# Block products for four more groups of joint tiles, and ScalarE durations by form in a kernel's list scheduler

## The chip, the cores and the metric

One core of a Trainium2 chip. The time is device microseconds of one execution, given as the median of several; the program runs on a single core, and every run used here is recorded as a fast one, with a granted TensorE clock of 0.997 to 1.00. A profile is of one execution of its own; its span is about 2 us shorter than that execution's time.

## The reference, cut to what matters

```python
B, T, D, K, U = 2, 4000, 512, 5, 8
h  = gelu(conv(x, w1))[:, ::2, :]          # 5 taps, stride 2
f  = gelu(conv(h, w2))[:, ::2, :]          # 5 taps, stride 2: 1000 rows a batch
fe = f @ w_f ;  ge = g @ w_g
j  = tanh(fe[:, :, None, :] + ge[:, None, :, :])
out = j @ w_o                              # 2 x 1000 x 8 rows of 512
```

The last product has 16,000 rows. The kernel does it in 125 **joint tiles** of 128 rows, in between and after the second batch's convolutions.

## The kernel before

The kernel first writes down all operations in program order; a **list scheduler** then orders them per engine by estimated durations. A plain joint tile is four matmuls of 512 columns into one PSUM bank, an eviction by VectorE or ScalarE, and a store issued by the sync engine:

```python
def act(o, i, func, scale=1.0, bias=None, cost=None):
    ...
    pl.op("act", ..., cost or o.ap.free_size() * 0.83e-3 + 0.13)      # the scheduler's duration
...
def joint_tile(jt):
    c0 = jt * P
    ahead(c0 + P, 900)                      # tanh of the columns to come
    ...
    early = jt < U * T2 // P                # tiles 0..61
    s = jt % 4 if early else 4 + jt % NSLOT # store slot, each with its own semaphore
    for h in range(2 if last else 1):       # the last tile in two halves
        ...
        mm(v, [(j(k), wo_sb[k, cl]) for k in range(NK)], True, True)
        if h == 1 or (jt % 3 == 2 if early else jt % 6 == 5) and not last:
            act(o, v, ACT.Copy)             # eviction on ScalarE
        else:
            ...                             # eviction on VectorE
        send(c0, s, cl, ("sp", "act")[h])
```

Eight **groups** of four tiles in the tail (tiles 64 and up) are done by seven instead of eight products of 2 x 2 blocks: `sums` makes four combinations of the operand (here on POOL), and four steps do two, two, two and one product, each of four matmuls of 256 columns. A group takes three of the eight PSUM banks in its first step.

```python
def one():
    held.extend(banks.pop(0) for _ in range(3))
    x, y, z = held
    product(Ab(0, 0), Bb(0, 0), x, True)
    product(Sb(1), Tb(1), y, True)
    act(k1, v2(x), ACT.Copy)
    tt("dve", u2, v2(y), k1, add)
...
WQ = (16, 18, 20, 22, 24, 26, 28, 30)       # the groups; a plain tile follows each of their steps
while todo and todo[0] < 60:                # plain tiles that run before the first group
    joint_tile(todo.pop(0))
```

At the end the sync engine waits for the semaphore of each of the 16 store slots.

## Time and profile before

| | |
|---|---|
| time, median | 266.12 us (265.56 to 266.48) |
| span of the profiled execution | 264.1 us |
| TensorE busy | 256.8 us, 97% |
| VectorE, ScalarE busy | 207.1 and 184.3 us |
| first joint tile's weight load | 88.90 us |
| start of the last eviction | 260.31 us |

The prediction below shows the page, the chain and the windows. Two views also belong here. The first is the list of waits of TensorE's weight loads between 150 and 258 us (columns: who waited for whom, us in total, times, longest):

```profile
PEld acc L424 <- DVE ostq L411: 0.9, 2, 0.5
PEld acc L424 <- ACT kq L416: 0.4, 2, 0.2
PEld acc L424 <- issue: 0.2, 1, 0.2
```

Here the weight loads ran ahead of the matmuls, so not all of the 1.3 us of the first two lines is lost; the starts of the matmuls show 0.47 us of lost time at 215.2, 218.2, 222.0 and 238.1 us. The second is the timeline of the end (start, length, what):

```profile
258.59 1.69 PE L424 MATMUL acc<-wo_sb,jL 128*128 128x512 bf16 x11
259.87 0.42 DVE L1059 CAST ostq<-acc 128x256 bf16<-128x256 f32 x1 [0.39 <-PE acc L424]
260.31 0.38 ACT L416 ACTIVATE ostq<-acc 128x256 bf16<-128x256 f32 x1 [0.28 <-DVE ostq L1059]
...
257.49 4.15 SPq L1038 DMA_DIRECT2D out_dram<-ostq  x8
```

The sync engine issues eight stores until 261.64 us with hardly a pause; the last ones begin 0.48 to 0.49 us apart. Store issue lags behind the evictions there.

### The profile page before, as it was taken

To read this page: it belongs to the slowest core of one execution; us is meant where nothing else is said; L and a number is where in the kernel's file an instruction comes from. 1 tells how busy PE (TensorE), PEld (TensorE's weight loads), DVE (VectorE), ACT (ScalarE), POOL (GpSimd) and SP (SyncE) were. 2 spreads that over 40 slices of the span, in tenths; PEclk is the share of its full clock that TensorE was granted. 3 is DMA by queue.
4 is the path that set the end of the run, shared out by engine and by line. 5 is a ranking of instruction groups with operands and counts; after the bars stand their busy time and mean duration, and the time that the engine had idled before them with its cause. 6 is when DMAs were issued, how large, how long until landed. Compare 5 with 4: busy or idle time off the path is not lost.

```text
span 264.1 us, 4593 instructions
## 1 busy us (share of the span) xinstructions
PE 256.8 (97%) x1658; PEld 161.3 (61%) x1678; DVE 207.1 (78%) x379; ACT 184.3 (70%) x305; POOL 43.3 (16%) x52
## 2 busy tenths in 40 slices
PE   8999999999999899999999999999999999999994
PEld 4887764456666555655655545555665666666662
DVE  0999999999999999994324999854345687887883
ACT  2788979984466999567547578738449999996111
POOL 1000005100000000000000000000003979698000
PEclk9999999999999999999999999999999999999998
DMA  6999998979993021211111113321101354445445
GB/s 239 327 180 218 293 260 147 171 128 194 227 183 62 20 83 58 79 40 62 41 60 40 63 60 119 123 80 60 61 21 40 123 159 159 161 142 179 160 160 159
DMA packets 56708, 33.94 MB, mean 129 GB/s; under 512 B 31582, under 2 KB 56430, under 8 KB 56686
## 3 DMA queue, kind: packets, MB, share of 16 engines
q1 hardware_dynamic: 54430, 31.49, 44.9%
q0 software_dynamic: 2112, 2.10, 4.6%
q8 instruction: 13, 0.21, 0.4%
q14 instruction: 9, 0.07, 0.1%
q10 hardware_dynamic: 144, 0.07, 0.1%
HBM read 7.86 MB, written 16.38 MB: 92 GB/s over the span
## 4 chain that ended last, share of the span: by engine, by line
PE 79%; DVE 14%; ACT 3%; issue 2%; DVEq 0%; ACTq 0%
PE acc L424 78%; DVE wide L411 2%; DVE r L592 2%; DVE r32b L592 2%; ACT w_t L416 1%; DVE ws L592 1%; DVE hT L411 1%; ACT jT L416 1%; PE acc L517 1%; DVE feT L988 1%; DVE sd L592 1%; DVE wide L741 1%; DVE row L592 1%; DVE row L741 1%; DVE acc L592 1%
## 5 line engine op out<-in xcount | busy, mean ns | idle before, releaser
L424 PE MATMUL acc<-wo_sb,jT 128*128 128x512 bf16 x242 | 60.5, 379 | 1.4 <-ACT jT L416 0.7
L1059 DVE CAST ost<-acc 128x512 bf16<-128x512 f32 x42 | 28.8, 688 | 19.6 <-PE acc L424 18.2
L416 ACT ACTIVATE jT<-feT,geT 128x1000 bf16<-128x1000 f32 (+9 forms) x56 | 40.9, 777 | 3.9 <-PE acc L424 2.4
L424 PEld LDWEIGHTS acc<-wo_sb,jT 128*128 128x128 bf16 x256 | 24.9, 98 | 23.8 <-ACT jT L416 0.8
L424 PE MATMUL acc<-wo_sb,jL 128*128 128x512 bf16 (+1 forms) x178 | 36.0, 336 | 0.3
L416 ACT ACTIVATE jL<-feT,geT 128x1000 bf16<-128x1000 f32 (+3 forms) x36 | 34.6, 1030 | 0.6 <-DVE feT L988 0.6
L1096 POOL TENSOR_TENSOR sA<-jL 128x512 f16<-128x512 bf16 x16 | 18.5, 1156 | 94.4 <-ACT jL L416 94.2
L424 PEld LDWEIGHTS acc<-wo_sb,jL 128*128 128x128 bf16 x184 | 17.8, 98 | 10.5 <-ACT kq L416 0.4
L424 PE MATMUL acc<-xt,w_sb 128*128 128x252 bf16 (+1 forms) x144 | 23.5, 305 | 0.0
L416 ACT ACTIVATE sd<-acc 128x334 f32<-128x334 f32 (+1 forms) x32 | 13.8, 443 | 11.8 <-PE acc L424 11.6
L416 ACT ACTIVATE hT<-acc 128x334 bf16<-128x334 f32 (+3 forms) x33 | 15.1, 464 | 9.1 <-PE acc L424 9.0
L1059 DVE CAST ostq<-acc 128x512 bf16<-128x512 f32 (+1 forms) x26 | 17.5, 678 | 4.1 <-PE acc L424 4.0
L424 PE MATMUL acc<-row,w_sb 128*128 128x334 bf16 (+1 forms) x112 | 20.5, 305 | 0.0
L424 PEld LDWEIGHTS acc<-xt,w_sb 128*128 128x128 bf16 x144 | 14.0, 98 | 7.0 <-DVE xt L411 0.3
L424 PE MATMUL acc<-zx,w_sb 128*128 128x334 bf16 (+1 forms) x96 | 17.6, 305 | 0.0
L411 DVE TENSOR_TENSOR ostq<-acc,kq 128x512 bf16<-128x512 f32 x24 | 15.7, 682 | 1.6 <-PE acc L424 1.6
L411 DVE TENSOR_TENSOR sd<-sd 128x334 f32<-128x334 f32 (+1 forms) x16 | 8.0, 503 | 10.7 <-ACT sd L416 10.7
L416 ACT ACTIVATE ost<-acc 128x512 bf16<-128x512 f32 x20 | 11.8, 592 | 5.0 <-PE acc L424 4.7
L424 PEld LDWEIGHTS acc<-row,w_sb 128*128 128x128 bf16 x112 | 10.9, 98 | 6.2
L424 PE MATMUL acc<-row,w_t 128*128 128x334 bf16 (+1 forms) x80 | 14.6, 305 | 0.0
L424 PE MATMUL acc<-xs,w_t 128*128 128x252 bf16 (+1 forms) x76 | 14.0, 314 | 0.3 <-issue 0.3
L416 ACT ACTIVATE ostq<-acc 128x512 bf16<-128x512 f32 (+1 forms) x14 | 8.2, 589 | 8.7 <-PE acc L424 8.2
(105 smaller groups left out, 469.1 us busy)
## 6 DMA issues: line engine op xcount, KB each, us to landing
out_dram<-ost SPq DMA_DIRECT2D x55, 128.0 KB, 1.9
out_dram<-ostq SPq DMA_DIRECT2D x54, 128.0 KB, 2.0
w_sb<-in_w_dram SPq DMA_DIRECT2D x10, 512.0 KB, 5.8
xr<-in_x_dram SPq DMA_DIRECT2D x2, 512.0 KB, 4.0
half<-w_sb POOLq DMA_DIRECT2D x2, 512.0 KB, 6.4
half<-w_t POOLq DMA_DIRECT2D x2, 512.0 KB, 5.2
wf_sb<-in_w_f_dram SPq DMA_DIRECT2D x1, 512.0 KB, 6.9
wg_sb<-in_w_g_dram SPq DMA_DIRECT2D x1, 512.0 KB, 5.4
```

The lines of the kernel that those rows point to most:

```text
L411: pl.op(eng, lambda e: e.tensor_tensor(out=o.ap, in0=a.ap, in1=b.ap, op=op), (a, b), (o,), vec_cost(o, (a, b)))
L416: pl.op("act", lambda e: e.activation(o.ap, i.ap, func, scale=scale, bias=0.0 if bias is None else bias.ap), rd, (o,), cost or o.ap.free_s ...
L424: ins = e.matmul(o.ap, lhsT=l.ap, rhs=r.ap, start=start and n == 0, stop=stop and n == len(pairs) - 1, skip_group_check=not check)
L517: ins = e.transpose(pv.ap[:, r, k, :], xr[rt].h[:, 2 * r + pp, k, :], ident.h[:, :])
L592: pl.op(eng, lambda e: e.scalar_tensor_tensor(out=o.ap, in0=a.ap, scalar=f, in1=b.ap, op0=ALU.mult, op1=op), (a, b), (o,), vec_cost(o, (a, ...
L741: pl.op("dve", lambda e: e.scalar_tensor_tensor(out=o.ap, in0=a.ap, scalar=-1.0, in1=b.ap, op0=ALU.mult, op1=sub), (a, b), (o,), vec_cost( ...
L988: pl.op("dve", lambda e, o=o, v=v: e.tensor_copy(out=o.ap, in_=v.ap), (v,), (o,), 0.47)
L1059: pl.op("dve", lambda e, o=o, v=v: e.tensor_copy(out=o.ap, in_=v.ap), (v,), (o,), vec_cost(o, (v,)))
L1096: pl.op(eng, lambda e, v=v, a=a, b=b, op=op: e.tensor_tensor(out=v.ap, in0=a.ap, in1=b.ap, op=op), (a, b), (v,), cost)
```

## The change

It wants fewer matmul columns on TensorE: four more groups (tiles 40 to 55) between the units of the second batch's second convolution. With it come other places for the eight late groups, other store slots and shares of the evictions, and ScalarE durations by form in the scheduler. The diff, cut:

```diff
+    WQ = (10,11,12,13,16,18,20,21,23,25,26,28)
+    LEAD = 6
-                  cost or o.ap.free_size() * 0.83e-3 + 0.13)
+                  cost or o.ap.free_size() * 0.84e-3 + (0.05 if i.psum else 0.17 if i.ap.dtype == FP32 else 0.09))
...
-            early = jt < U * T2 // P
-            s = jt % 4 if early else 4 + jt % NSLOT
+            early = jt < LATE                     # 30
+            s = jt % 4 if early else (0, 12, 1, 13, 2, 14, 3, 15)[plain[0] % 8]
...
-                if h == 1 or (jt % 3 == 2 if early else jt % 6 == 5) and not last:
+                if h == 1 or (jt % 3 == 2 if early else plain[0] % 3 == 2) and not last:
...
+        for q in WQ:                              # steps of groups and plain tiles in one work list
+            late = q >= 16
+            st = quad_steps(q, "pool" if late else "dve")
...
+            while late and left and left[0] < 52 + LEAD:
+                todo.append((lambda jt=left.pop(0): joint_tile(jt), 1))
+            todo.insert(max(len(todo) - 3, 0), (st[0], 0))
+            for f in st[1:]:
+                todo.append((f, 1))
+                if late and left:
+                    todo.append((lambda jt=left.pop(0): joint_tile(jt), 1))
...
+        weights_o()                               # moved ahead of the convolution units
         joint(6)
```

`joint(n)` now takes n pieces from that work list, be they plain tiles or group steps. The sums of the new groups are on VectorE. Three plain tiles end the kernel where one did.

More of the change, by code (lines that the diff above doesn't have):

```diff
@@ L341, in bass_standalone__seq2seq_rnn_t_joint__speech_kernel @@
     RING, LRING = 2048, 4096
-    FROM = 64 * P
+    WQ = (10,11,12,13,16,18,20,21,23,25,26,28)
+    LEAD = 6
+    FROM, LATE = 64 * P, 30
     NSLOT = 12
@@ L394, in bass_standalone__seq2seq_rnn_t_joint__speech_kernel @@
         sA = [at(f"sA{i}", [4, 2, 2 * P], FP16, 16384 + i * 4096) for i in range(3)]
-        kq = [at(f"kq{i}", [3, 2, 2 * P], FP32, o) for i, o in enumerate((28672, Q[0]))]
+        kq = [at(f"kq{i}", [3, 2, 2 * P], FP32, o) for i, o in enumerate((28672, X[2] + 8192, Q[0]))]
         ostq = at("ostq", [NSLOT, NT], BF16, 0)
@@ L996, in tanh @@
                     n = min(hi - lo, RING - lo % RING, FROM - lo)
+                    assert done.issuperset(range(max(lo - RING, 0) // P, (lo + n - RING + P - 1) // P)), lo
                     o = jT[k][lo % RING:lo % RING + n]
@@ L999, in tanh @@
                     n = min(hi - lo, LRING - lo % LRING)
+                    assert done.issuperset(range(max(lo - LRING, FROM) // P, (lo + n - LRING + P - 1) // P)), lo
                     o = jL[k, lo % LRING:lo % LRING + n]
@@ L1012, in bass_standalone__seq2seq_rnn_t_joint__speech_kernel @@
         pend, state = [], [0, 1]
+        work = []
+        done, plain = set(), [0]
         def joint(count):
-            for _ in range(count):
-                joint_tile(state[0])
-                state[0] += 1
+            while work and count > 0:
+                f, n = work.pop(0)
+                f()
+                count -= n
         def ahead(c1, more):
@@ L1042, in joint_tile @@
             c0 = jt * P
+            done.add(jt)
             ahead(c0 + P, 900)
@@ L1046, in joint_tile @@
             j = lambda k: jL[k, r0:r0 + P] if late else jT[k][r0:r0 + P]
-            early = jt < U * T2 // P
-            s = jt % 4 if early else 4 + jt % NSLOT
+            early = jt < LATE
+            s = jt % 4 if early else (0, 12, 1, 13, 2, 14, 3, 15)[plain[0] % 8]
+            plain[0] += not early
             last = jt == ntile - 1
@@ L1054, in joint_tile @@
                 mm(v, [(j(k), wo_sb[k, cl]) for k in range(NK)], True, True)
-                o = ost[s][cl] if early else ostq[s - 4, cl]
-                if h == 1 or (jt % 3 == 2 if early else jt % 6 == 5) and not last:
+                o = ost[s][cl] if s < 4 else ostq[s - 4, cl]
+                if h == 1 or (jt % 3 == 2 if early else plain[0] % 3 == 2) and not last:
                     act(o, v, ACT.Copy)
@@ L1072, in quad_steps, with A @@
             c0 = 4 * q * P
-            r0, S_, (k1, u2, k15) = c0 % LRING, sA[u[0] % 3], [kq[u[0] % 2][i] for i in range(3)]
+            late = c0 >= FROM
+            r0, S_ = c0 % (LRING if late else RING), sA[u[0] % 3]
+            k1, u2, k15 = [kq[u[0] % (3 if late else 2)][i] for i in range(3)]
             u[0] += 1
-            A = lambda i, j: jL[2 * j:2 * j + 2, r0 + 2 * i * P:r0 + 2 * (i + 1) * P]
+            def A(i, j, k=None):
+                lo = r0 + 2 * i * P
+                if late:
+                    return jL[2 * j:2 * j + 2, lo:lo + 2 * P] if k is None else jL[2 * j + k, lo:lo + 2 * P]
+                return jT[2 * j + k][lo:lo + 2 * P]
             v2 = lambda b: ps.cols(b * NT, NT).map(lambda a: a.rearrange("p (t c) -> p t c", t=2))
@@ L1081, in product, with Ab @@
                     mm(ps.cols(bk * NT + 256 * t, 256), [(a(k, sl), b(k)) for k in range(2)], start and t == 0, True, False)
-            Ab = lambda i, j: lambda k, sl: jL[2 * j + k, r0 + 2 * i * P + sl.start:r0 + 2 * i * P + sl.stop]
+            def Ab(i, j):
+                lo = r0 + 2 * i * P
+                if late:
+                    return lambda k, sl: jL[2 * j + k, lo + sl.start:lo + sl.stop]
+                return lambda k, sl: jT[2 * j + k][lo + sl.start:lo + sl.stop]
             Sb = lambda i: lambda k, sl: S_[i, k, sl]
@@ L1086, in quad_steps @@
             Tb = lambda i: lambda k: wT[i, k]
-            s0 = 4 * (q % 3)
+            s0 = 4 * (u[0] % 2)
             half = lambda i, j: ostq[s0 + 2 * i:s0 + 2 * i + 2, 256 * j:256 * j + 256]
@@ L1091, in sums @@
             def sums():
-                ahead(c0 + 4 * P, 900)
-                cost = 1.2 if eng == "pool" else 0.331
-                for o, a, b, op in ((0, A(1, 0), A(1, 1), add), (2, A(0, 0), A(1, 0), sub), (1, S_[0], A(0, 0), sub), (3, A(0, 1), S_[1], sub)):
-                    v = S_[o]
-                    pl.op(eng, lambda e, v=v, a=a, b=b, op=op: e.tensor_tensor(out=v.ap, in0=a.ap, in1=b.ap, op=op), (a, b), (v,), cost)
+                ahead(c0 + 4 * P, 900 if late else 300)
+                for k in (None,) if late else range(2):
+                    w = 2 if late else 1
+                    cost = (0.58 if eng == "pool" else 0.133) * w + (0 if eng == "pool" else 0.065)
+                    S1 = lambda i: S_[i] if late else S_[i, k]
+                    for o, a, b, op in ((0, A(1, 0, k), A(1, 1, k), add), (2, A(0, 0, k), A(1, 0, k), sub), (1, S1(0), A(0, 0, k), sub),
+                                        (3, A(0, 1, k), S1(1), sub)):
+                        v = S1(o)
+                        pl.op(eng, lambda e, v=v, a=a, b=b, op=op: e.tensor_tensor(out=v.ap, in0=a.ap, in1=b.ap, op=op), (a, b), (v,), cost)
             def one():
@@ L1126, in four @@
                 product(Ab(1, 1), Tb(3), y, False)
+                done.update(range(4 * q, 4 * q + 4))
                 tt("dve", half(1, 0), v2(y), k1, add)
@@ L1134, in bass_standalone__seq2seq_rnn_t_joint__speech_kernel @@
         fes = [1]
+        for jt in range(WQ[0] * 4):
+            work.append((lambda jt=jt: joint_tile(jt), 1))
+        left = [jt for jt in range(WQ[0] * 4, ntile) if jt // 4 not in WQ]
+        todo = []
+        for q in WQ:
+            late = q >= 16
+            st = quad_steps(q, "pool" if late else "dve")
+            n = len(work)
+            first_w = len(todo) == 0
+            while late and left and left[0] < 52 + LEAD:
[5 more added lines that the diff above has]
+                    todo.append((lambda jt=left.pop(0): joint_tile(jt), 1))
+        work.extend(todo)
+        work.extend((lambda jt=jt: joint_tile(jt), 1) for jt in left)
         for h in range(2):
@@ L1199, in bass_standalone__seq2seq_rnn_t_joint__speech_kernel @@
         fes[0] = 2
-        weights_o()
-        WQ = (16, 18, 20, 22, 24, 26, 28, 30)
-        steps = {}
-        n0 = state[0]
-        todo = [jt for jt in range(n0, ntile) if jt // 4 not in WQ]
-        quads = [quad_steps(q, "pool") for q in WQ]
-        done = 0
-        for i, q in enumerate(quads):
-            pass
-        while todo and todo[0] < 60:
-            joint_tile(todo.pop(0))
-        quads[0][0]()
-        for i, q in enumerate(quads):
-            if i + 1 < len(quads):
-                pass
-            for f in q[1:]:
-                f()
-                if todo:
-                    joint_tile(todo.pop(0))
-                if f is q[1] and i + 1 < len(quads):
-                    quads[i + 1][0]()
-        while todo:
-            joint_tile(todo.pop(0))
+        joint(len(work))
         pl.emit(block, [(s[0], s[1]) for s in slot_sem])
```

## The prediction

> **What bounds the kernel now.** I read the page's busy shares first, then the slices.
>
> ```profile
> PE 256.8 (97%) x1658; PEld 161.3 (61%) x1678; DVE 207.1 (78%) x379; ACT 184.3 (70%) x305; POOL 43.3 (16%) x52
> PE   8999999999999899999999999999999999999994
> DVE  0999999999999999994324999854345687887883
> ACT  2788979984466999567547578738449999996111
> ```
>
> TensorE looks busy everywhere, VectorE only in the first 18 slices (to about 118 us), ScalarE in slices 31 to 36. A busy share does not say whether TensorE is at its best rate, so I read the chain of work that ended last, from 86 us on.
>
> ```profile
> 88.86 0.27 issue
> 89.14 9.96 PE acc L424 x55
> 99.09 0.05 issue
> 99.14 8.07 PE acc L424 x49
> ...
> 125.23 10.37 PE acc L424 x65
> ```
>
> Before 89 us this chain runs mostly through VectorE (transforms of the convolution operands). From 89.14 to 259.87 us, where the last eviction begins, it is TensorE without a real gap: 170.7 us, 65% of the span. What is taken from TensorE there should come off the time; what is added to another engine there is free while TensorE does not wait for it.
>
> Is TensorE at its full rate there? The timeline of TensorE around 224 us shows both kinds of work side by side:
>
> ```profile
> 223.55 0.60 PE L424 MATMUL acc<-wT,sA 128*128 128x256 f16 x4
> 223.99 0.60 PE L424 MATMUL acc<-wo_sb,sA 128*128 128x256 bf16 x4
> 224.43 1.03 PE L424 MATMUL acc<-wo_sb,jL 128*128 128x512 bf16 x4
> 225.29 0.60 PE L424 MATMUL acc<-wT,jL 128*128 128x256 f16 x4
> ```
>
> Columns are start, length, and what; lengths overlap, so I take starts. Eight 256-column matmuls take 224.43 - 223.55 = 0.88 us (0.110 each), four of 512 columns 225.29 - 224.43 = 0.86 us (0.215 each). Over all neighbours in the trace the median start-to-start is 216 ns (512 columns), 109 ns (256) and 142 ns (334). Counted from the code, the work from about 86 us on is 93 plain tiles (372 matmuls x 216 = 80.4 us), 8 block groups (8 x 28 x 109 = 24.4), 288 + 144 convolution matmuls (432 x 142 = 61.3) and 48 of the last feature projection (6.8): 172.9 us, of which about 3.4 us ran before 89.14. That leaves 169.5 us of demand in 170.7 us of time. TensorE is within 1% of its own rate, so only fewer matmul columns can help there.
>
> **What the Trainium skill says.** "Perfetto Trace Analysis", section "Identifying the Most-Contended Engine", warns that matmul busy share is a poor measure of headroom; agreed: the 512-column matmul is recorded with 379 ns but starts every 216. "TensorE: Matmul & The Clock Gate", section "Wait — 56ns, not 53.3ns?", gives N/2.4 GHz plus about 2.5 ns from start to start when warm: 215.8 and 109.2 ns; the trace has 216 and 109 at a granted clock of 1.00. "VectorE: DVE Perf Modes", section "The perf-mode tier table (the rule you actually need)", lets a two-tensor operation on 16-bit data in SBUF run at two elements per cycle but one with a PSUM operand at one; agreed: 334-element 16-bit operations start every 243 ns, 512-element evictions every 601. "ScalarE: Activation LUTs", section "What ACT_TABLE_LOAD costs", charges about 93 ns more for a pointer bias; the 1000-element tanh starts every 1019 ns, where 1000 x 0.833 plus 93 plus the copy's fixed part fits.
>
> **The change part by part.**
>
> *Fewer matmul columns.* A block group does four joint tiles with 7 products of 2 x 2 matmuls of 256 columns: 28 x 109 = 3.052 us, against 16 x 216 = 3.456 us for four plain tiles. Groups go from 8 to 12 (tiles 40 to 55, in four groups, are new; the late ones are still eight, at other places). Gain: 4 x 0.404 = **1.62 us**, all on the path.
>
> *More eviction and sums.* Each new group is evicted by 5 VectorE and 2 ScalarE operations where four plain tiles had about 2.7 and 1.3. VectorE: 2.3 x 0.60 = 1.4 us more, plus 8 sums of 256 elements (from the 334-element rate, 243 - 78/1.92 = 202 ns each) = 1.6 us: 3.0 us per group, 12 us in all. Preparing the combined output weights (4 x 0.42 = 1.7 us) also moves from after the feature projection to before these groups. ScalarE gets about 0.3 us per group. Where does this lie? By counting weight loads, tile 40 begins at 165.9 us and tile 53 at 200.4:
>
> ```profile
> 172.00:201.00 29.00, 28.79 (x182) 17.97 (x185) 13.52 (x26) 16.54 (x29) 1.16 (x1) 1.00 0.15 50
> 201.00:217.00 16.00, 15.95 (x97) 9.37 (x97) 10.71 (x18) 16.00 (x23) 11.96 (x11) 1.00 0.38 124
> ```
>
> Columns: stretch, its length, busy time of PE, weight loads, VectorE, ScalarE, POOL. VectorE is 13.5 of 29 us busy, so 12 us fit, tightly. On the path: 0, with up to 0.4 us for late evictions.
>
> *The tail.* Late plain tiles go from one eviction in six on ScalarE to one in three: about 12 instead of 5 or 6 there, 6 x 0.48 = 2.9 us more ScalarE. ScalarE is full from 201 to 217 us but only 28.0 of 43 us in the rest, and the extra ones lie all over. Its first block group also comes sooner: after the projection TensorE has one group step and tiles 56 to 61 that need no tanh of the second batch, 0.43 + 6 x 0.86 = 5.6 us, where it had tiles 55 to 61, 6.0 us. Cost: 0 to 0.5 us; I take 0.2.
>
> *Scheduler durations of ScalarE.* They change only the order. Old formula for 512 elements from PSUM 0.555 us, new 0.480, trace 0.477; 334 elements 0.407, 0.331, trace 0.329; 1000 fp32 elements from SBUF 0.96, 1.01, trace 1.019. The new ones are right. An order made with them may shave something off the first 89 us, where TensorE issues only about 81 us of columns (194,000 / 2400) and VectorE is 82 of 89 us busy; or shuffle it the other way. I take -0.3 us, a guess from that slack, uncertain by 1.
>
> Sum: -1.62 + 0.2 (early stage) + 0.2 (tail) - 0.3 (order) = -1.5; I put the changed kernel at 266.12 - 1.7 = **264.4 us**, leaning a little to the gain since both mid-stage costs may be nil.
>
> **Rivals.**
>
> *PSUM banks become the bound.* In the convolution stage up to five of the eight banks are held by units in flight, and a group holds three from its first step to its last: eight of eight. A bank freed by an eviction is then taken again one step later. For: plain tiles had three banks to rotate, now there is no spare. Against: a convolution step between group steps is eight matmuls (1.1 us) or more, an eviction 0.6 to 0.7. If it bit at each of 16 steps by 0.1 to 0.3 us, the gain would vanish: 264.5 + 1.6 to 4.8 = 266 to 269.
>
> *The tanh ring.* The ring for the first batch holds 16 tiles. The last tanh of that batch overwrites tiles 39 to 46 and so waits for the second new group, while the fourth needs it complete and then summed: 4 x 1.02 + 8 x 0.2 = 5.7 us. Tile 48 starts at 180.8 and tile 52 at 191.6 us now, so about 11 us are there. Speaks against; if it came late, TensorE would take the feature projection first. Cost 0 to 1 us.
>
> *ScalarE in the tail.* If tanh for the second batch falls behind by the added evictions, the waits at 201 to 217 us grow: up to 2.9 us, time 265 to 267.
>
> *The new order helps the front more than thought.* Of the about 8 us that TensorE does not issue before 89 us most is start-up, the fixed 2.5 ns of each matmul and operands on VectorE; 1 to 2 us could come back: 262.5 to 263.5.
>
> **Range and chances.** The sure term is 1.6 us; the order at the front and the waits in the middle are each worth about a microsecond either way. Range 262.6 to 266.1. Two per cent is 5.3 us: faster by that would need three times the sure gain (0.03); slower by that would need the bank rival and the tail rival together (0.02); within 2% 0.95.
>
> **What would show it.** Right: 112 more and 64 fewer matmuls by form (48 more in all); the stage from tile 40 to the projection's end shorter by about 1.2 to 1.6 us; the chain from the first joint tile still TensorE with only 0.05 us issue pieces; VectorE near 25 of 29 us in that stage; the last matmul's distance to the end unchanged at about 4.2 us. Wrong: waits of TensorE's weight loads on VectorE or ScalarE of over 1 us between 165 and 220 us (banks, ring or tail), or the first joint tile moving by over 1 us from 88.9 (the order, not the products, decides).

## The result

The changed kernel took 262.65 us (262.49 to 263.11, 4 runs) against 265.98 us of the kernel before in the same rounds: ratio 0.9877, interval 0.9855 to 0.9899. A ratio is the mean time of one kernel's runs over that of the other's of the same rounds, so not quite the ratio of the medians. That is within 2%, as forecast, but the gain was 3.3 us where 1.7 were forecast.

Two lines of the changed kernel's page, then three of its chain:

```profile
PE 255.1 (98%) x1726; PEld 165.6 (64%) x1726; DVE 215.9 (83%) x415; ACT 188.0 (72%) x313; POOL 43.1 (17%) x52
DVE  1999999999999999995243999999937877777774
```

```profile
88.31 0.05 issue
88.35 169.29 PE acc L426 x1112
257.66 0.38 ACT ost L418
```

In the VectorE row, slices 26 to 29 (about 163 to 189 us) read 9, 9, 9, 9 where before they read 8, 5, 4, 3: there the new groups' sums and evictions lie. The chain from the first joint tile to the last eviction is one single piece of 1,112 matmuls. In the trace of before it was cut by "issue" pieces of 0.05 us; those are no waits. At each of them one matmul record is lost: 1,658 matmuls stand against 1,678 weight loads (the twentieth is the very first matmul of the first joint tile), and the neighbours of each gap start one 512-column matmul (216 ns) further apart. In the changed kernel's trace none is lost.

```profile
172.00:201.00 29.00, 29.00 (x221) 21.25 (x219) 23.47 (x58) 19.98 (x34) 1.16 (x1) 1.00 0.19 60
201.00:217.00 16.00, 16.00 (x111) 10.77 (x110) 11.77 (x19) 16.00 (x25) 13.28 (x12) 1.00 0.46 150
```

VectorE, the third engine, goes from 13.52 to 23.47 of 29 us. TensorE does not wait for it there: the view of its weight loads' waits from 150 to 258 us, which had the three lines above, is empty. The granted clock is 1.00 in all stretches of both kernels up to 258 us, so it has no part in the difference. The end:

```profile
257.51 0.33 SPq L1046 DMA_DIRECT2D out_dram<-ostq  x1
257.89 0.43 SPq L1046 DMA_DIRECT2D out_dram<-ost  x1
258.08 0.37 ACTq L1046 DMA_DIRECT2D out_dram<-ost  x1
```

The sync engine has 0.29 us free before the first of its last two stores, and the last store of all is ScalarE's half tile, 0.41 us after its eviction began: no backlog. To see where 3.5 us of span (264.09 to 260.60) went I cut both at two marks, the first weight load of a joint tile and the start of the last eviction:

| us | before | changed | difference |
|---|---|---|---|
| until the first joint tile | 88.90 | 88.35 | -0.55 |
| from there to the last eviction | 171.41 | 169.31 | -2.10 |
| from there to the end | 3.78 | 2.94 | -0.84 |

In the middle, columns / 2.4 GHz plus 2.5 ns for each matmul but the last (the lost records added) give 170.42 us of demand before and 168.84 changed, while the matmul starts span 171.1 and 169.0 us. That rate is the one of the Trainium skill, "TensorE: Matmul & The Clock Gate", section "Wait — 56ns, not 53.3ns?"; the changed kernel's trace keeps to it within 0.16 us in 169. So 1.6 us are columns, and about 0.5 us are waits that TensorE had before and has no longer.

### The profile page after: what moved, and what is told of

It reads as the page before. It is cut to its first block, busy times and chain, and to the rows that moved or that the text cites. A ratio compares the mean times of both kernels' runs of the same rounds, so it can differ in the third digit from the quotient of the medians. Undisturbed runs are those within 1.5% of the kernel's fastest.

```text
span 260.6 us, 4764 instructions
## 1 busy us (share of the span) xinstructions
PE 255.1 (98%) x1726; PEld 165.6 (64%) x1726; DVE 215.9 (83%) x415; ACT 188.0 (72%) x313; POOL 43.1 (17%) x52
## 4 chain that ended last, share of the span: by engine, by line
PE 83%; DVE 12%; ACT 2%; issue 1%; DVEq 0%; ACTq 0%
PE acc L426 83%; DVE wide L413 2%; DVE r L594 2%; DVE r32b L594 2%; DVE hT L413 1%; ACT jT L418 1%; DVE feT L990 1%; DVE sd L594 1%; PE acc L519 1%; DVE sd L413 1%; DVE wide L743 1%; DVE row L743 1%; DVE row L594 1%; DVE zx L413 0%; ACT w_sb L418 0%
## 5 line engine op out<-in xcount | busy, mean ns | idle before, releaser
L426 PE MATMUL acc<-wo_sb,jT 128*128 128x512 bf16 (+1 forms) x224 | 52.5, 364 | 0.6 <-ACT jT L418 0.6
L426 PE MATMUL acc<-wo_sb,jL 128*128 128x512 bf16 (+1 forms) x184 | 36.9, 337 | 0.0
L418 ACT ACTIVATE jL<-feT,geT 128x1000 bf16<-128x1000 f32 (+3 forms) x36 | 35.3, 1046 | 0.6 <-DVE feT L990 0.6
L1069 DVE CAST ost<-acc 128x512 bf16<-128x512 f32 (+1 forms) x37 | 25.2, 687 | 10.0 <-PE acc L426 10.0
L426 PEld LDWEIGHTS acc<-wo_sb,jT 128*128 128x128 bf16 x224 | 21.7, 98 | 18.2 <-ACT jT L418 1.0
L413 DVE TENSOR_TENSOR ostq<-acc,kq 128x512 bf16<-128x512 f32 x36 | 23.6, 684 | 3.1 <-PE acc L426 3.1
L426 PE MATMUL acc<-xt,w_sb 128*128 128x252 bf16 (+1 forms) x144 | 23.5, 305 | 0.0
L413 DVE TENSOR_TENSOR kq<-acc,kq 128x512 f32<-128x512 f32 x24 | 16.1, 686 | 7.7 <-ACT kq L418 6.8
L426 PE MATMUL acc<-wT,sA 128*128 128x256 f16 x144 | 21.3, 273 | 0.0
L426 PEld LDWEIGHTS acc<-wT,sA 128*128 128x128 f16 x144 | 14.1, 98 | 5.5
L418 ACT ACTIVATE ostq<-acc 128x512 bf16<-128x512 f32 x20 | 12.2, 611 | 5.6 <-PE acc L426 5.4
```

The lines of the kernel that those rows point to most:

```text
L413: pl.op(eng, lambda e: e.tensor_tensor(out=o.ap, in0=a.ap, in1=b.ap, op=op), (a, b), (o,), vec_cost(o, (a, b)))
L418: pl.op("act", lambda e: e.activation(o.ap, i.ap, func, scale=scale, bias=0.0 if bias is None else bias.ap), rd, (o,), cost or o.ap.free_s ...
L426: ins = e.matmul(o.ap, lhsT=l.ap, rhs=r.ap, start=start and n == 0, stop=stop and n == len(pairs) - 1, skip_group_check=not check)
L1069: pl.op("dve", lambda e, o=o, v=v: e.tensor_copy(out=o.ap, in_=v.ap), (v,), (o,), vec_cost(o, (v,)))
```

## The experiments

All ran five timed rounds beside the kernel before, and each left a profile. Where the first loads land differs between executions, so I judge by the pieces above, which repeat better than the times. The end is cut further: from the last eviction's start to the issue of the last store, to its landing, to the end of the program.

**The changed kernel again.**

> The changed kernel itself, so that the other runs of this call have it on the same chip. Theory from the two traces (gain 3.5 us of span = 2.05 in the stage bound by TensorE + 0.85 after the last eviction + 0.6 before the first joint tile): 262.4 to 263.1, ratio to before 0.986 to 0.990. If the 0.6 us at the front is only when the first loads land, the first weight load of a joint tile moves between profiles by some tenths of a microsecond.

263.35 us (262.44 to 263.87) against 265.73, 2.4 us less; ratio 0.9892 (0.986 to 0.9924). Its first joint tile came at 89.29 us, 0.94 later than in the first profile, and later than before's 88.90; the middle was 169.31 and the end 2.95 us, as in the first. The front piece is chance. TensorE transposes two freshly loaded blocks near the start of the program; from the last of those to the first joint tile it is 81.34 us (before), 81.38 and 81.37 (changed), while that last transpose itself (its weight load) began at 7.56, 6.97 and 7.92 us. So the front difference of 0.55 us belongs to the loads; about 2.9 us of span are the change's.

**Without the new groups.**

```diff
+            if not late:
+                todo.extend((lambda jt=jt: joint_tile(jt), 1) for jt in range(4 * q, 4 * q + 4))
+                continue
```

> The changed kernel with the four new groups given back as 16 plain tiles, all else kept. Theory: only the matmul columns come back, 4 x 0.404 = 1.6 us over the changed kernel, so 264.2. Rival (the new groups gain more than their columns, for they take evictions or waits along; or less, for the banks make TensorE wait): back to 265 or more, or under 263.6.

264.69 us, 1.34 over the changed kernel. Middle 171.00 us, with 0.12 us of waits in it; end 2.85. The groups are worth 171.00 - 0.12 - 169.31 = 1.57 us beside waits, their columns and no more.

**The late groups at their old places.**

```diff
-    WQ = (10,11,12,13,16,18,20,21,23,25,26,28)
-    LEAD = 6
+    WQ = (10,11,12,13,16,18,20,22,24,26,28,30)
+    LEAD = 8
```

> The changed kernel with the late groups at their old places (one plain tile last in place of three, tiles to 59 ahead of the first late group). Theory: the stores pile up again behind the last evictions, span after the last eviction 3.8 us in place of 2.9, time +0.6 to +1.2 over the changed kernel: 263.3 to 263.9. Rival (the short end is chance of that execution): same as the changed kernel within 0.3 us.

263.09 us, in time the same as the changed kernel. Its middle is the same (169.30), its end longer by 0.5: 3.45 us, of which 0.69 to the last issue (0.41 in the changed kernel), 2.10 to the landing (1.86) and 0.66 after it. By the times alone the rival would hold; in the profiles the longer end is hidden by the front, for the last transpose began at 7.18 us against 7.92. The theory had 0.6 to 1.2 us; it is the lower edge or less, and not all of the end.

**The old ScalarE durations.** One line is undone, the `cost` of `act`.

> The changed kernel with the scheduler's old ScalarE durations. Theory A (the new durations give an order without the 0.47 us of waits at 215 to 238 us and help the front): +0.5 to +1.1 us, 263.2 to 263.8. Theory B (order by old durations is as good): within 0.3 us of the changed kernel.

263.51 us. From the transposes to the first joint tile 81.33 us, as with the new ones: theory A's help at the front is refuted. The middle is 169.83, with 0.48 us of waits, almost all at 212.2 and 232.0 us: theory A's other half holds. The waits of TensorE's weight loads from 200 to 258 us:

```profile
PEld acc L426 <- ACT kq L418: 0.7, 2, 0.4
PEld acc L426 <- DVE ostq L413: 0.2, 1, 0.2
```

**The new ScalarE durations alone, on the kernel before.**

> The kernel before with the new ScalarE durations alone. Theory A: the order gives 0.5 to 1.1 us by itself, 264.9 to 265.5, with less than 0.2 us of waits of TensorE after 200 us. Theory B: within 0.3 us of before, and first joint tile at 88.5 to 89.

265.33 us against 266.16, ratio 0.9973. Front again unchanged (81.34 us after the transposes). Middle 171.02 in place of 171.41, waits 0.13 in place of 0.47 us. The end, 3.78 us, is unchanged. The waits of the weight loads from 200 to 258 us:

```profile
PEld acc L424 <- DVE ostq L411: 0.7, 2, 0.5
```

So the durations are worth 0.3 to 0.5 us of waits in the tail and, in these profiles, nothing elsewhere.

**The late groups at the new places, on the kernel before.** `WQ` as the changed kernel has it from 16 on, and `todo[0] < 58`.

> The kernel before with the late groups at the new places and two plain tiles less ahead of them, so three plain tiles end it. Theory: the end after the last eviction shrinks by 0.85 us and part of the waits at 215 to 238 us goes: 264.6 to 265.3. Rival: the short end needs the new store slots or evictions too: no change within 0.3 us.

265.92 us against 266.16, ratio 0.9989 (0.9968 to 1.0009): the rival. Waits 0.47 us as before, now at 221 and 225; end 3.82 us. Three plain tiles at the end do not help by themselves. From 254.40 us on VectorE does nine evictions one after the other, ScalarE only one and the final half, and eleven stores are issued back to back from 255.72 to 260.98 us. Only one plain tile in six goes to ScalarE here, but that alone is not the reason: in the run with one in six below, ScalarE has nothing but the final half in the last 5.9 us, and the last store is still issued 0.41 us after the last eviction begins.

**Two queues for the stores of the last group, on the kernel before.**

```diff
-                    send(c0 + t * P, 4 + s0 + t)
+                    send(c0 + t * P, 4 + s0 + t, eng="act" if q == 30 else "sp")
```

> The kernel before, the four stores of the last block group sent from ScalarE's queue in place of the sync engine's. Theory: the end is long because one queue issues the last seven stores at 0.48 us each until 261.64 us, 0.95 us after the last eviction; with two queues the end shrinks by 0.4 to 0.9 us: 265.2 to 265.7. Rival: the transfers themselves are at their rate (about 131 KB per 0.5 us in the last 3 us), and a second queue changes nothing: 266.0.

265.49 us against 266.16 (ratio 0.9981, 0.9961 to 1.0001). The last store is issued 0.41 us after the last eviction in place of 0.84, but lands 2.24 us later in place of 1.94; the end is 3.66 us. Both theories have a part. The 130 KB or so that land in each half microsecond of the last 3 us of transfers of the kernel before are no limit of the transfers: it is what one queue issues (128 KB each 0.49 us), and with two queues 156 to 165 KB land in some of them. But then a store takes longer to land. And the last eviction itself comes 0.15 us later after the last matmul than before. ScalarE's queue is issuing stores until 0.10 us ahead of it; that this holds it up is argued:

```profile
258.90 0.85 ACTq L1038 DMA_DIRECT2D out_dram<-ostq  x2
259.85 0.38 ACT L416 ACTIVATE ostq<-acc 128x256 bf16<-128x256 f32 x1 [0.43 <-DVE ostq L1059]
```

From the end of the last matmul to the end of the program it is 3.85 us, against 3.82 before: nothing is gained in the profile, and its shorter span is the front's (first joint tile at 88.30 against 88.90 us). The Trainium skill, "DMA: Bandwidth & Descriptors", section "Issuing engines are not separate DMA queues", says that a second issuing engine saves only issue time; here it saved 0.43 us of that, of which the landing left 0.12 and the later eviction none.

**One plain eviction in six on ScalarE.** `plain[0] % 3 == 2` becomes `plain[0] % 6 == 5`.

> The changed kernel with one plain eviction in six on ScalarE after tile 30, as late tiles had before, in place of one in three. Theory: the waits of TensorE in the second batch's tail come back in part, +0.2 to +0.6 us: 262.9 to 263.3; VectorE near its full time from 165 to 200 us. Rival: no wait comes back, within 0.2 us of the changed kernel.

262.52 us, the best time of all, by an early start: its first joint tile came at 87.98 us. This is not the loads alone: from the last transpose it is 81.09 us, 0.3 less than in the changed kernel, with VectorE's work before it in another order. The two runs with more early groups below have 81.04 us, so an order can be worth 0.3 us at the front. The middle is 169.81 us. Against the theory the tail's waits did not come back (0.05 us at 231 and 237). But one wait of 0.42 us appeared at 171.8 us, among the new groups, where TensorE has two steps of groups back to back that have four convolution matmuls between them in the changed kernel. My edit also cuts the share of tiles 30 to 61, which had been one in three in both kernels; that this made the scheduler order it so is argued:

```profile
165.00:180.00 15.00, 14.75 (x119) 11.10 (x117) 15.00 (x42) 8.74 (x15) 0.00 (x0) 1.00 0.15 49
```

VectorE is busy all 15 us there, as in the changed kernel, and ScalarE 8.74 us against 9.74.

**The last tile's store in another slot, on the kernel before.**

```diff
-            early = jt < U * T2 // P
+            early = jt < U * T2 // P or jt == ntile - 1
```

> The kernel before, its last tile stored from slot 0 in place of slot 8. Theory: the closing waits are made one by one, about 63 ns each, and slot 8's comes first, so that eight more follow the last landing; slot 0's comes last. From the last landing to the end 0.5 us in place of 0.99, the stage up to the last eviction unchanged at 171.4: time -0.5 us, 265.5. Rival (those waits run beside the landing, the end is set by something else): no change of that piece.

265.48 against 265.77 us, ratio 0.9996 (0.9974 to 1.0018): too small for the times. The pieces are clear: middle 171.39, to the last issue 0.83, to the landing 2.06, and from the landing to the end 0.49 us in place of 1.00. The records of the sync engine's closing waits in the kernel before (time, semaphores; slot 0 has 121, slot 8, the last tile's, 129):

```
263.10  129
263.16  130 and 128
263.23  131 and 127
 ...    one more every 63 ns
263.53  136 and 122
263.60  121, then the common end of the program
```

The first of them is the one that waits for the last store; the others have long been met, and are still gone through one by one. In the changed kernel the last tile has slot 3 (semaphore 124), the sixth in this row, and 0.66 us are left after the landing; 1.00 - 0.66 = 0.34 us of the gain.

**The new groups only.** The changed kernel with the old places, old durations and old shares.

> The four new groups with the late groups' places, the scheduler's durations and the shares of evictions as in the kernel before. Theory: from the first joint tile to the last eviction 171.4 - 1.6 = 169.8, with the 0.47 us of waits of TensorE still there; end 3.45 us (the new store slots keep 0.35 us of gain at the closing waits); time 264.0 to 264.5, near what the products alone were forecast to give. Rival (the groups also take away waits): stage 169.3.

263.98 us against 265.77, ratio 0.9925 (0.9911 to 0.9939). Middle 169.72, waits 0.39 us (four, from 220 to 235), end 3.38 us: 0.84 to the last issue as before, 0.66 after the landing. This is what the prediction described: the products alone, with nothing lost and nothing else won but the slot.

**A fifth and a sixth early group.** `WQ` begins with 9, then with 8; both have the last tile in slot 0.

> The changed kernel with a fifth early group (tiles 36 to 39) and the last tile in slot 0. Theory: one group more is 0.404 us of TensorE, the slot 3 x 0.063 = 0.19 us of closing waits: stage 168.9, end 2.75, time -0.6 against the changed kernel, 262.0 to 262.4. Rival: VectorE, full from 160 to 180 us, makes TensorE wait at 160 to 175 us, stage 169.3 or more.

265.54 us, ratio 0.9991: the rival. TensorE's demand falls by 0.4 us as it should, but 2.2 us of waits stand between 158 and 178 us; the view names VectorE for 2.0 us of its weight loads' waits and ScalarE for 1.6:

```profile
153.00:180.00 27.00, 25.91 (x180) 16.74 (x180) 27.00 (x77) 19.01 (x33) 0.00 (x0) 1.00 0.24 79
```

VectorE is busy for all 27 us there, and so it already is in the changed kernel, but not in the kernel before (changed, then before):

```profile
153.00:180.00 27.00, 27.00 (x185) 17.74 (x184) 27.00 (x76) 20.39 (x34) 0.00 (x0) 1.00 0.21 68
153.00:180.00 27.00, 26.84 (x153) 14.99 (x155) 22.35 (x55) 18.62 (x33) 0.00 (x0) 1.00 0.26 89
```

The changed kernel sits at the edge: VectorE full, TensorE not waiting yet. The middle was 172.30 us; beside the waits, the last eviction began 1.4 us after the last matmul, where it is 0.3 in the changed kernel. With fewer plain tiles the slots fall otherwise, and slot 0 had been used two plain tiles earlier. The eviction waited for that store, a flaw of my edit:

```profile
260.66 0.42 DVE L1069 CAST ost<-acc 128x256 bf16<-128x256 f32 x1 [1.25 <-DMA out_dram<-ost]
```

> The same with a sixth early group too (tiles 32 to 35). Theory: another 0.40 us of TensorE if its sums come in time, stage 168.5, time 261.6 to 262.0. Rival: the group's sums must wait until the first convolution's weights at their place are last read (about 153 us) and for VectorE, which is busy with the transforms there; then TensorE waits before 165 us and the gain is gone.

267.09 us, ratio 1.0054, slower than the kernel before: 4.9 us of waits between 155 and 180 us, VectorE 27.00 of 27 us. I ran no version that beats the changed kernel clearly. It with the last tile in slot 0 alone should gain 0.66 - 0.49 = 0.17 us, an estimate from the pieces above, under what the times resolve.

## Why the prediction was right or wrong

"Within 2%" was right, and so was the bound; the size was not: 1.7 us forecast, 3.3 measured in the medians (2.4 when measured again), 2.9 without the chance of the loads.

- *Fewer matmul columns, 1.62 us on the path*: right. 1.57 us when taken away alone, 1.6 us in the count of the traces. The forms are as forecast: 112 more matmuls of 256 columns, 64 fewer of 512, counting the lost records.
- *More eviction and sums, up to 0.4 us*: right in place, nothing on the path. VectorE's 23.5 of 29 us compares with "near 25". What the forecast read from a mean of 29 us hides that VectorE is full from 153 to 180 us in the changed kernel; one group more cost over 2 us of waits. The forecast also saw VectorE busy "only in the first 18 slices", but the row that it shows has three more nines in slices 23 to 25: from 145 to 165 us VectorE is busy 19.97 of 20 us in the kernel before. That four groups still fit is in part luck.
- *The bank rival, the ring rival, ScalarE in the tail*: did not happen. TensorE has no wait over 15 ns from the first joint tile on, though ScalarE is still busy all 16 us from 201 to 217 us. The bank rival was also overstated: a group does not keep its three banks to its last step.
- *The tail, 0.2 us of cost*: wrong in sign. The forecast saw 170.7 us for 169.5 us of demand and called the rest "within 1%" of the rate. Its sum is off: 16 of the convolution and projection matmuls ran before the first joint tile (2.3 us, not 3.4), and the demand counted in the traces is 170.4 us of 171.1. Of the 0.7 us left, 0.47 were waits that could go. They go with the new durations: 0.13 us left when those are put into the kernel before, 0.48 back when they are taken out of the changed one. The forecast had found the new durations right (0.480 against a measured 0.477 us) and then looked for their worth in the wrong stage.
- *Scheduler durations, -0.3 us in the first 89 us*: wrong. From the last transpose to the first joint tile it is 81.3 us with either formula, in four kernels. Three other orders had 81.0 to 81.1 us, so there was something to win, but not by the durations.
- *"the last matmul's distance to the end unchanged at about 4.2 us"*: this is the step that failed most, 0.84 us of the 1.2 that were missing. From the start of the last matmul to the end it is 4.09 us before and 3.24 changed. The forecast took the end as fixed latency. It held 0.43 us of stores waiting for the issuing queue and 0.34 us of closing waits that follow the last landing, and the change altered both: the first by when the last evictions come and where, the second by the slot number of the last tile.

The account without the front: 1.6 (columns) + 0.5 (waits) + 0.43 (store issue) + 0.08 (landing) + 0.34 (closing waits) = 2.9 us, beside 3.78 + 171.41 - 2.94 - 169.31 = 2.94 us.

What stays open: which part shortens the store issue. The old places account for 0.28 of the 0.43 us (0.69 against 0.41); the old durations and shares together for the rest (0.84 against 0.69), and the new places alone, on the kernel before, bring nothing (0.93), so at least two parts must come together. With the new places kept, neither the old durations nor one eviction in six alone bring the backlog back (0.41 both times). Open too is how the durations' order avoids the waits, and what in the order moves the front by 0.3 us.

## What to carry to other kernels

Where one engine runs at its own rate, count what it must do and how long it takes to the tenth of a microsecond: the difference is a gain that a change of order can bring beside the one that is meant. Cut the time after the last compute instruction into issue, landing and closing waits before calling it fixed; here each of the three changed with choices in the kernel. And when parts of a kernel differ by less than the scatter of its start, compare the pieces between two marks, not the times.

## What the Trainium skill lacked or had wrong

- I found no page with the cost of closing waits that are already met: 63 ns for each, one by one, so the order of semaphores against the order of landings was worth 0.5 us here (1.00 to 0.49 us by a change of slot).
- "DMA: Bandwidth & Descriptors", section "Issuing engines are not separate DMA queues", calls the issue time usually small relative to the transfer. For one store that is so here (0.49 us from one issue to the next, about 2 us from issue to landing), but the section does not say that issues add up: back to back they made the last store 0.43 us late (0.84 us from the last eviction to the last issue, 0.41 with two queues).
- "Perfetto Trace Analysis" does not tell that matmul records can be lost one at a time: 20 of 1,678 in the trace of before, 19 of them leaving a gap that is 216 ns longer and shows as a 0.05 us "issue" piece. Weight loads per matmul tell them from waits.
